# Wv's load and the clearing of z's buffer, moved in the start of a four-layer kernel

## The chip, the core and the metric

The kernel runs on one core of a Trainium2 chip. Five engines work side by side, each with its own queue: PE (TensorE) multiplies matrices, DVE (VectorE), ACT (ScalarE) and POOL (GpSimd) work on elements, and SP (SyncE) issues the transfers, which 16 DMA engines carry out. Engines wait for each other by counters (semaphores). The metric is the time of one execution on the device in microseconds; lower is better.

## The reference

Two kinds of layer, a linear attention (A) and an MLP (B), are run as A, B, A, B on 2048 tokens of 576 features, with the same weights in both turns. Weights and inputs are bf16.

```python
def _A_ref(x, wqkv, wo):              # S = 2048, D = 576, H = 32 heads of 18
    qkv = (x @ wqkv).reshape(B, S, 3, H, Dh).transpose(2, 0, 3, 1, 4)
    q, k, v = qkv[0], qkv[1], qkv[2]
    phi = lambda t: jnp.where(t > 0, t + 1, jnp.exp(t)) + 1e-6
    pq, pk = phi(q), phi(k)
    kv = jnp.einsum("bhsd,bhse->bhde", pk, v)
    z = jnp.einsum("bhsd->bhd", pk)
    num = jnp.einsum("bhqd,bhde->bhqe", pq, kv)
    den = jnp.einsum("bhqd,bhd->bhq", pq, z)[..., None] + 1e-6
    return (num / den).transpose(0, 2, 1, 3).reshape(B, S, D) @ wo

def _B_ref(x, w1, b1, w2, b2):        # F = 4608
    y = _layernorm(x, axis=-1)
    h = _gelu(jnp.einsum("bsd,df->bsf", y, w1) + b1)
    return jnp.einsum("bsf,fd->bsd", h, w2) + b2

x = A_x
x = x + _A_ref(_layernorm(x, axis=-1), A_wqkv, A_wo)
x = x + _B_ref(_layernorm(x, axis=-1), B_w1, B_b1, B_w2, B_b2)
x = x + _A_ref(_layernorm(x, axis=-1), A_wqkv, A_wo)
x = x + _B_ref(_layernorm(x, axis=-1), B_w1, B_b1, B_w2, B_b2)
```

## The kernel before

**Tiling.** Tokens go in 16 tiles of 128 (t = 0 to 15), and in four chunks of 512 for the queries. Features are cut into five pieces of up to 128 (index k). The normalised, transposed tokens stand in `yT`.

**The weights of a layer A** stand in one buffer, `wqkv_sb`, 128 partitions by 5 pieces k by 1736 columns. In each piece columns 0 to 583 hold Wq, 584 to 1159 Wk (`KO` = 584) and 1160 to 1735 Wv (`VO` = 1160). Wq is laid out in four groups of 128 columns, 126 of weights and two more, and a last group of 72 columns. The two more columns of each group are copies of the last eight of those 72: `fill_groups` (L239 to L246) makes them with two copies on POOL at L242, one over pieces 0 to 3 and 128 partitions, one over piece 4 and 64 partitions. The first product with Wq (`q_proj`, PE L708) reads such a group.

**The beginning of the first layer** is written out by hand. SP's queue: token tiles 0 to 2 (L214), Wk in two halves (L223, L225), tiles 3 and 4, Wq in five pieces (L234) and two for the last columns (L236, L238), tiles 5 to 15, and then Wv in three transfers (L223, L225 and L261: the lower half of piece 4 is loaded a second time into the upper 64 partitions). Behind these come pieces of w1 (L285), which alternate with transposes of tiles 8 to 15 by the DMA (L547). Every DMA counts on one of eight counters in turn, and waits until the DMA eight places before it, which used the same counter, has landed.

Tiles 0 to 3 are normalised on DVE, tiles 4 to 15 on POOL (L481 a power, L489, L495, in layer A one tile after the other). PE computes the keys of a tile (`k_half`, L740), ACT and DVE make pk of them (L608, L610), and PE sums, over a tile's tokens, x times pk (`rows_by_keys`, L786). Such a sum for a tile reads one more column of `pk` that POOL sets to 1 (L746). Between the tiles lie the products with Wq (`q_proj`, L708), whose results ACT and DVE turn into pq (L630, L634, L640, L642).

The hand-written order around the change is: keys of tiles 0 and 1, the sums of tile 0, keys of tile 2, `fill_groups()`, the sums of tiles 1 and 2, keys of tile 3, the first `q_proj`, the transposition of tile 4 (L558), the second `q_proj`, the sums of tile 3, and then a loop over tiles 4 to 15. Besides these orders, waits come from what the instructions read and write: an instruction that touches a region of a buffer waits for the earlier ones of the program that touch an overlapping region. The region of the first copy of L242 reaches from piece 0 to piece 3, so that columns of Wk and Wv lie inside it.

**z's buffer.** z, the sum of pk over all tokens, is collected in `zk`, which is the first of three ring buffers, `y_ring[0]`. The ring serves the first tiles' exponentials too. In `rows_by_keys` POOL clears half of `zk` at the last tile (L802, 128 by 288), and ACT writes one row into it behind that. The scheduler places this clearing on POOL's queue where its buffer is free: behind L746's columns of tiles 1 and 2 and ahead of L242.

The rest of layer A (sums for the second half of the keys, denominators, the product with Wo at L1105) and the layers B (L1220, L1216, L1284) follow in PE's order.

Of the kernel before, what the change touches and what calls it, by code (L numbers as in the profile page):

```python
# [14 lines left out]
S, D, F, H, DH = 2048, 576, 4608, 32, 18  # L15
P = 128
# [11 lines left out]
KO, VO = QW, QW + D  # L28
# [12 lines left out]
def build(tc, A_x, A_wqkv, A_wo, B_w1, B_b1, B_w2, B_b2, out, dbg=None, n_layers=4):  # L41
    nc = tc.nc
    dbg = dbg or {}
    with ExitStack() as ctx:
# [102 lines left out]
        wqkv_sb = const.tile([P, KD, QW + 2 * D], BF16, name="wqkv_sb")  # L147
# [36 lines left out]
        def chained(inst):  # L184
            if chain["last"] is not None:
                tc.add_manual_dep(inst.ins, chain["last"], NOSYNC, reason="start-up DMA issue order")
            chain["last"] = inst.ins.name
            return inst
# [30 lines left out]
        def load_wqkv(part, half=None):  # L219
            cols = slice(part * D, (part + 1) * D) if half is None else \  # L220
                slice(part * D + half * HALF, part * D + (half + 1) * HALF)
            home = slice(cols.start + QW - D, cols.stop + QW - D)
            chained(nc.sync.dma_start(out=wqkv_sb[:, 0:4, home],  # L223
                                      in_=A_wqkv[0:4 * P, cols].rearrange("(k p) n -> p k n", p=P)))
            chained(nc.sync.dma_start(out=wqkv_sb[0:64, 4, home], in_=A_wqkv[4 * P:D, cols]))  # L225
# [30 lines left out]
        load_wq()  # L256
        for t in range(5, NT):
            load_x0(t)
        load_wqkv(2)

        chained(nc.sync.dma_start(out=wqkv_sb[64:P, 4, VO:VO + D], in_=A_wqkv[4 * P:D, 2 * D:3 * D]))  # L261
        nc.vector.memset(y_ring[NY - 1][:, 0:P], 0.0)
        warm_ps = ps_h.tile([P, 512], F32, name="warm_ps", tag="h")

# [54 lines left out]
        pool_last = dict(norm=None)  # L319
# [374 lines left out]
        def layer_A(li, next_kind, pre_a1=None):  # L694
# [39 lines left out]
            zk = y_ring[0][:, 0:D]  # L734
# [38 lines left out]
            def rows_by_keys(t, half, chunks=(4, 0, 1, 2, 3), done=True):  # L773

                if t == 0 and 0 in chunks:
                    self_k["acc"] = [ps_acc.tile([P, 2, 512], F32, name="k2_ps", tag=tag) for tag in ("accA", "accB")]
                if t == 0 and 4 in chunks:
                    self_k["tail"] = ps_h.tile([P, 512], F32, name="k2_tail", tag="h")
                summed = li == 0 and half == 0
                n = HALF + summed  # L780
                pk = self_k["pk"][(0, t)][:, 0:n] if summed else \
                    self_k["pk"][(half, t // 2)][:, (t % 2) * HALF:(t % 2 + 1) * HALF]
                for k in chunks:
                    dst = self_k["tail"][0:65, 0:n] if k == 4 else self_k["acc"][k // 2][:, k % 2, 0:n]
                    lhsT = row_of[t][:, 4 * P:D + 1] if k == 4 else row_of[t][:, k * P:(k + 1) * P]
                    pe(nc.tensor.matmul(dst, lhsT=lhsT, rhs=pk, start=(t == 0), stop=(t == NT - 1)))  # L786
                cols = slice(half * HALF, (half + 1) * HALF)
                if summed and t == NT - 1:
                    for i in range(2):
                        nc.vector.tensor_scalar(out=key_eps[:, 2 * i:2 * i + 2].unsqueeze(2),  # L790
                                                in0=self_k["acc"][i][:, :, HALF:HALF + 1], scalar1=1e-6, scalar2=None,
                                                op0=ALU.mult)
                    for rows_, col in ((slice(0, 64), 4), (slice(64, 65), 5)):
                        nc.vector.tensor_scalar(out=key_eps[rows_, col:col + 1], in0=self_k["tail"][rows_, HALF:HALF + 1],
                                                scalar1=1e-6, scalar2=None, op0=ALU.mult)
                if done and t == NT - 1:
                    for i, engine in enumerate((nc.scalar, nc.vector)):
                        for j in range(2):
                            plus_eps(engine, k2[2 * i + j][:, cols], self_k["acc"][i][:, j, 0:HALF],
                                     key_eps[:, 2 * i + j:2 * i + j + 1])  # L800
                if 4 in chunks and t == NT - 1:
                    nc.gpsimd.memset(zk[:, cols], 0.0)  # L802
                    plus_eps(nc.scalar, k2[4][0:64, cols], self_k["tail"][0:64, 0:HALF], key_eps[0:64, 4:5])
                    plus_eps(nc.scalar, zk[64:65, cols], self_k["tail"][64:65, 0:HALF], key_eps[64:65, 5:6])
                if not done:
                    return
                if summed:
                    del self_k["pk"][(0, t)]
                elif t % 2:
                    del self_k["pk"][(half, t // 2)]  # L810
                if half:
                    del row_of[t]
                    if li == 0 and t == NT - 1:
                        x0_tiles.clear()
# [162 lines left out]
            if li == 0:  # L977
                def keys(t):
                    k_half(t, 0)
                    k_half(t, 1)  # L980


                def feed_and_tick(t, n):
                    feed0(t, after=dve_last["phi"] if t > 5 else None)
                    for _ in range(n):
                        lnp.tick()

                k_half(0, 0)
                lnp.tick()
                phi = k_half(0, 1, defer=True)  # L990
                k_half(1, 0)
                feed_and_tick(3, 2)
                k_half(1, 1)
                phi()
                rows_by_keys(0, 0, (0, 1, 2, 3), done=False)
                keys(2)
                fill_groups()
                feed_and_tick(4, 2)
                rows_by_keys(1, 0, (0, 1, 2, 3), done=False)
                rows_by_keys(2, 0, (0, 1, 2, 3), done=False)  # L1000
                k_half(3, 1)
                k_half(3, 0)
                q_proj(*q_left.pop(0))
                feed_and_tick(5, 1)
                feed_and_tick(6, 2)
                phi = q_proj(*q_left.pop(0), defer=True)
                lnp.tick(transposes=0)
                first_max = phi(after=first_ones["ca4"].ins.name, late=True)
                in_order("s0a s0b g0 s1a s1b n0 g1 s2a cd0 n1 s2b g2 u2 cd1 n2 ma00 s3a s3b g3 u3 ma10 ma01 n3 ma11 ma20 "
                         "s4a s4b g4 u4 ma21 ma31 s5a ma30 s5b g5 u5")  # L1010
                in_order("ln0 re0 ln1 re1 ca0 e00 ca1 e01 e10 ca2 e11 e20 e21 ca3 e31 e30 ca4")
                rows_by_keys(3, 0, (0, 1, 2, 3), done=False)
                for t in range(4, NT):
                    if t in (4, 5):
                        k_half(t, 0)
                        (first_max if t == 4 else largest)(dve_after=dve_last["phi"])
                        k_half(t, 1)
                        if t == 4:
                            in_order("u5 s6a s6b g6 u6 ma40 ma41")
                    else:  # L1020
                        keys(t)
                    pre_a1(t)
                    if t == 4:
                        lnp.tick(transposes=0)
                    masks(2)
                    if t > 4:
                        rows_by_keys(t - 1, 0)
                    else:
                        for one in range(4):
                            rows_by_keys(one, 0, (4,))  # L1030
                    behind_keys = act_last["turned"] if t <= XB or act_last["stats"] is None else act_last["stats"]
                    if t != 6:
                        largest = q_proj(*q_left.pop(0), defer=True)(after=behind_keys, late=t == 4)
                    lnp.tick(transposes=0)
                q_proj(*q_left.pop(0))
                rows_by_keys(NT - 1, 0)
                masks(len(mask_steps))
            else:
                for t in range(6, NT - TPC):
                    load_row(t)  # L1040
                for t in range(NT):

                    if t >= 4:
                        pre_a1(t)
                    k_half(t, 0)
                    if t >= 7:
                        pre_a1(t)
                    k_half(t, 1)
                    if t > 1:
                        q_proj(*q_left.pop(0))  # L1050
                    if t:
                        rows_by_keys(t - 1, 0)
                rows_by_keys(NT - 1, 0)
# [341 lines left out]
```

## Time and profile before

| | us |
|---|---|
| median of 3 runs | 763.77 (762.59 to 764.33) |
| profiled execution | 764.52 |
| span of its instructions | 762.8 |
| PE busy | 748.5 (98%) |
| PE's longest wait, for POOL's copy at L242 | 7.7 |
| ACT, DVE, POOL busy | 315.0, 261.1, 119.3 |
| DMA, share of 16 engines | 35% |

The span runs from the first to the last instruction of the core. PE's clock can be granted in part; the profile gives it as a share of full speed, 0.993 in the mean here. A timeline's row gives the start, the time, the engine, the line, the operation and, in brackets, how long the engine sat idle before it and what ended that. A row of the chain of waits gives start, time and instruction; the chain is followed back from the last instruction of the span. In a row of windows stand the stretch, its length, the busy time of PE, PE's weight loads, DVE, ACT and POOL with the number of instructions, the granted clock, the DMA's busy share and the GB/s that it moved.

### The profile page before, as it was taken

What the parts mean: (1) busy time and instruction counts of PE and PEld (TensorE: products, weight loads), DVE (VectorE), ACT (ScalarE), POOL (GpSimd) and SP (SyncE); (2) the same over time, 40 slices, a digit from 0 to 9 for tenths busy, and PEclk for the clock granted to TensorE, in tenths of its full rate; (3) what the DMA queues carried; (4) which work ended last, traced back from release to release, by engine and by line L of the source; (5) the groups of instructions that cost most, each with busy time, mean ns of one, the idle gap of its engine ahead of it and who ended that gap; (6) DMA issues with size and microseconds to landing.
All of it is one profiled execution on the core that took longest, in us unless ns stands there. A gap on an engine that the chain in (4) does not pass through costs nothing.

```text
span 762.8 us, 15695 instructions
## 1 busy us (share of the span) xinstructions
PE 748.5 (98%) x6536; PEld 475.8 (62%) x6536; DVE 261.1 (34%) x645; ACT 315.0 (41%) x703; POOL 119.3 (16%) x231
## 2 busy tenths in 40 slices
PE   6899999999999999999999999999999999999998
PEld 4566664675477447745776667447745764674476
DVE  6465764045213603300357667600240032000000
ACT  3566747403620570065037766570064036205600
POOL 2670323012100301110100004200020011001000
PEclk9799999999999999999999999999999999999999
DMA  8299496315502631230413047530241033011000
GB/s 217 80 242 227 154 274 221 83 47 158 142 19 65 183 83 40 94 87 1 141 40 86 33 126 262 205 83 16 65 107 36 16 125 82 9 32 56 2 9 24
DMA packets 88546, 75.73 MB, mean 99 GB/s; under 512 B 45002, under 2 KB 73114, under 8 KB 88474
## 3 DMA queue, kind: packets, MB, share of 16 engines
q1 hardware_dynamic: 88474, 74.72, 34.6%
q8 instruction: 51, 0.84, 0.5%
q14 instruction: 21, 0.17, 0.1%
HBM read 48.10 MB, written 24.77 MB: 96 GB/s over the span
## 4 chain that ended last, share of the span: by engine, by line
PE 93%; SPq 1%; ACT 1%; DMA 1%; DVE 1%; POOL 1%; issue 1%; POOLq 0%; ACTq 0%; DVEq 0%
PE m_ps L1284 36%; PE h_ps L1220 20%; PE hp_ps L1220 16%; PE wo_ps L1105 5%; PE q_ps L708 4%; PE k_ps L740 4%; PE k_ps L786 3%; PE m_half L1284 1%; SPq L214 1%; DMA w_sb<-in_B_w_dram 1%; PE q_ps L713 1%; DMA wqkv_sb<-in_A_wqkv_dram 1%; ACT turned L966 1%; PE k_tail L786 0%; PE rden_ps L962 0%
## 5 line engine op out<-in xcount | busy, mean ns | idle before, releaser
L1284 PE MATMUL m_ps<-w_sb,hT 128*128 128x288 bf16 x2232 | 274.8, 286 | 0.0
L1284 PEld LDWEIGHTS <-hT 128*128 128x128 bf16 x2304 | 224.3, 98 | 60.4 <-issue 3.4
L1220 PEld LDWEIGHTS <-w_sb 64*128 64x128 bf16 x2304 | 124.4, 94 | 136.7 <-issue 1.9
L1220 PE MATMUL hp_ps<-yT,w_sb 64*128 64x512 bf16 x1152 | 178.0, 376 | 0.0
L1220 PE MATMUL h_ps<-yT,w_sb 64*128 64x512 bf16 x1152 | 148.0, 376 | 0.0
L1225 ACT COPY relay_sb<-relay_sb 128x1 f32<-128x1 f32 x144 | 28.6, 199 | 260.7 <-PE h_ps L1220 218.7
L1216 ACT ACTIVATE hT<-h_ps,b1T 128x512 bf16<-128x512 f32 x144 | 91.2, 684 | 44.7 <-PE h_ps L1220 44.7
L481 POOL TENSOR_TENSOR ln_rstd<-ln_u,neg_half 128x1 f32<-128x1 f32 x62 | 34.9, 563 | 371.6 <-DVE ln_u L463 215.7
L1216 ACT ACTIVATE hT<-hp_ps,b1T 128x512 bf16<-128x512 f32 x144 | 91.2, 693 | 0.0
L684 DVE TENSOR_TENSOR xbf<-m_ps,xo 128x576 bf16<-128x576 f32 x15 | 11.4, 758 | 212.0 <-PE m_ps L1284 212.0
L684 DVE TENSOR_TENSOR xo<-m_ps,xo 128x576 f32<-128x576 f32 x16 | 12.1, 758 | 167.5 <-PE m_ps L1284 167.5
L667 POOL TENSOR_TENSOR xo<-xo,b_bc 128x576 f32<-128x576 f32 x32 | 41.0, 1284 | 105.8 <-DMA xo<-x_d 92.3
L1220 PE MATMUL h_ps<-yT,w_tail 64*128 64x512 bf16 x144 | 54.1, 376 | 0.0
L1220 PE MATMUL hp_ps<-yT,w_tail 64*128 64x512 bf16 x144 | 54.1, 376 | 0.0
L708 PE MATMUL q_ps<-yT,wqkv_sb 128*128 128x512 bf16 x160 | 41.8, 395 | 7.7 <-POOL wqkv_sb L242 7.7
L740 PE MATMUL k_ps<-wqkv_sb,yT 128*128 128x288 bf16 x320 | 44.6, 286 | 0.2 <-ACT yT L564 0.2
L1105 PE MATMUL wo_ps<-kvwo,pq 128*128 128x288 bf16 x320 | 42.3, 286 | 0.2 <-DVE xn L684 0.2
L740 PEld LDWEIGHTS <-yT 128*128 128x128 bf16 x320 | 30.9, 98 | 11.4 <-issue 0.6
L1220 PEld LDWEIGHTS <-w_tail 64*128 64x128 bf16 x288 | 27.1, 94 | 17.1
L630 ACT ACTIVATE phi_e<-q_ps 128x512 bf16<-128x512 f32 (+1 forms) x38 | 21.6, 575 | 35.4 <-PE q_ps L708 32.4
L1105 PEld LDWEIGHTS <-pq 128*128 128x128 bf16 x320 | 30.6, 98 | 8.6 <-issue 0.4
L344 DVE STREAM_TRANSPOSE turned<-y_ring 128x576 bf16<-128x576 bf16 x40 | 30.4, 767 | 0.4
(161 smaller groups left out, 546.6 us busy)
## 6 DMA issues: line engine op xcount, KB each, us to landing
xo<-x_d SPq DMA_DIRECT2D x48, 288.0 KB
x_d<-xo SPq DMA_DIRECT2D x32, 288.0 KB
xl<-x_d SPq DMA_DIRECT2D x24, 288.0 KB
y_d<-turned SPq DMA_DIRECT2D x40, 144.0 KB
w_sb<-in_B_w_dram SPq DMA_DIRECT2D x6, 864.0 KB
yT<-y_d SPq DMA_DIRECT2D x10, 512.0 KB
w_sb<-in_B_w_dram SPq DMA_DIRECT2D x9, 512.0 KB
x_d<-xn SPq DMA_DIRECT2D x16, 288.0 KB
```

The costliest lines, as they stand in the source:

```text
L344: turn = nc.vector.transpose(out=turned[:, :, j, :], in_=y[:, 0:D])
L481: power = nc.gpsimd.tensor_tensor(out=rstd[:], in0=it["u"][:], in1=neg_half[:], op=ALU.pow)
L667: nc.gpsimd.tensor_tensor(out=xo[:], in0=xo[:], in1=b2_bc[:], op=ALU.add)
L684: total = nc.vector.tensor_tensor(out=xn[:, cols].rearrange("p (h n) -> p h n", h=2), in0=halves, in1=xo[:, cols].rearrange("p (h n) -> p ...
L708: pe(nc.tensor.matmul(qp[:], lhsT=wqkv_sb[:, k, g * P:(g + 1) * P], rhs=yT[:, k, c * CA:(c + 1) * CA], start=(k == 0), stop=(k == KD - 1)))
L740: pe(nc.tensor.matmul(kp[:, 0:HALF], lhsT=yT[:, k, t * P:(t + 1) * P], rhs=wqkv_sb[:, k, KO + half * HALF: KO + (half + 1) * HALF], start= ...
L786: pe(nc.tensor.matmul(dst, lhsT=lhsT, rhs=pk, start=(t == 0), stop=(t == NT - 1)))
L1105: pe(nc.tensor.matmul(wp[:, half, 0:HALF], lhsT=features, rhs=kvwo[slot][:, half * HALF:(half + 1) * HALF], start=(g == WO_ORDER[0]), stop ...
L1216: act_last["gelu"] = nc.scalar.activation(out=to, in_=ps, func=ACT.Gelu_apprx_tanh, bias=b1T[:, f:f + 1], scale=1.0).ins.name
L1220: mm = pe(nc.tensor.matmul(dst[n], lhsT=wt, rhs=mv, start=(seen[n] == 0), stop=(seen[n] == 8)))
L1225: relay = nc.scalar.copy(out=relay_sb[:, 1:2], in_=relay_sb[:, 0:1])
L1284: pe(nc.tensor.matmul(acc[half][:, 0:cols.stop - cols.start], lhsT=hT[f][:, j * P:(j + 1) * P], rhs=w2_sb[:, f, cols], start=(f == 0), sto ...
```

## The change

Two edits. The three transfers of Wv are issued by the same queue at the same place among the transfers, but stand in the program behind `fill_groups()`, so that what they must wait for, and what must wait for them, is worked out from there. And the clearing of `zk` in the first layer gets an order: behind the last tile that POOL has normalised at that point of the program.

```diff
         for t in range(5, NT):
             load_x0(t)
-        load_wqkv(2)
-
-        chained(nc.sync.dma_start(out=wqkv_sb[64:P, 4, VO:VO + D], in_=A_wqkv[4 * P:D, 2 * D:3 * D]))
+
+        def load_wv():
+            load_wqkv(2)
+            chained(nc.sync.dma_start(out=wqkv_sb[64:P, 4, VO:VO + D], in_=A_wqkv[4 * P:D, 2 * D:3 * D]))
+
...
                 if 4 in chunks and t == NT - 1:
-                    nc.gpsimd.memset(zk[:, cols], 0.0)
+                    cleared = nc.gpsimd.memset(zk[:, cols], 0.0)
+                    if li == 0:
+                        tc.add_manual_dep(cleared.ins, pool_last["norm"], NOSYNC, reason="tiles go on first")
                     plus_eps(nc.scalar, k2[4][0:64, cols], self_k["tail"][0:64, 0:HALF], key_eps[0:64, 4:5])
...
                 keys(2)
                 fill_groups()
+                load_wv()
                 feed_and_tick(4, 2)
```

`chained` keeps the order of the transfers on SP. `load_wqkv(2)` issues two of the three transfers, for pieces 0 to 3 and for piece 4.

In the two programs' instruction lists PE, DVE and ACT have the same instructions in the same order, and so has SP; on SP the first transfer of Wv now waits for POOL as well. On POOL three things stand elsewhere: the clearing of `zk` comes behind the last mask (L113) instead of ahead of L242, and one filling of an x buffer with ones (L277) and the two L746 columns of tiles 1 and 2, which stood ahead of L242, stand behind it.

## The prediction

> **What bounds the kernel now.** The page first: PE is busy for 98% of the span, so only an idle PE, or a slow one, can give time back. The slices show both at the beginning.
>
> ```profile
> PE 748.5 (98%) x6536; PEld 475.8 (62%) x6536; DVE 261.1 (34%) x645; ACT 315.0 (41%) x703; POOL 119.3 (16%) x231
> PEclk9799999999999999999999999999999999999999
> ```
>
> The granted clock falls below full only in the second slice of 19 us. Next PE's timeline over the first 28 us, where the bracket names the wait, and POOL's over the same stretch:
>
> ```profile
> 11.98 1.15 PE L786 MATMUL k_ps<-pk,x 128*128 128x289 bf16 x8
> 12.97 1.39 PE L740 MATMUL k_ps<-wqkv_sb,yT 128*128 128x288 bf16 x10
> 22.08 2.31 PE L708 MATMUL q_ps<-yT,wqkv_sb 128*128 128x512 bf16 x5 [7.73 <-POOL wqkv_sb L242]
> ```
>
> ```profile
> 10.84 0.14 POOL L746 MEMSET pk<- 128x1 bf16 x2
> 14.74 0.34 POOL L802 MEMSET y_ring<- 128x288 bf16 x1 [3.76 <-DMA x<-in_A_x_dram]
> 21.81 0.33 POOL L242 COPY wqkv_sb<-wqkv_sb 128x32 bf16<-128x32 bf16 x2 [6.73 <-DMA w_sb<-in_B_w_dram]
> 22.11 0.54 POOL L481 TENSOR_TENSOR ln_rstd<-ln_u,neg_half 128x1 f32<-128x1 f32 x1
> ```
>
> PE stands still from 14.36 (12.97 + 1.39) to 22.08, for a copy of 0.33 us that POOL begins at 21.81. POOL is free from 15.08 and waits 6.73 us for a DMA. The row names a w1 transfer, which the copy does not touch; the name is that of the latest issue on a shared counter. Of what the copy does touch or enclose, Wv is the last. Then the windows, for the clock and the bytes:
>
> ```profile
> 16.50:17.00 0.50, 0.00 (x0) 0.00 (x0) 0.00 (x0) 0.00 (x0) 0.00 (x0) 1.00 1.07 316
> 17.00:17.50 0.50, 0.00 (x0) 0.00 (x0) 0.00 (x0) 0.00 (x0) 0.00 (x0) 0.56 0.85 277
> 26.50:27.00 0.50, 0.50 (x3) 0.22 (x2) 0.38 (x2) 0.00 (x0) 0.00 (x0) 0.50 0.00 0
> 27.00:27.50 0.50, 0.50 (x5) 0.30 (x4) 0.00 (x0) 0.40 (x1) 0.00 (x0) 0.70 0.00 0
> ```
>
> The clock halves at about 17.05, 2.7 us after PE's last matmul, and is whole again at about 27.3, 5.2 us after PE resumes. Last the chain of waits, which shows what SP waits for and what PE's slow stretch leads to:
>
> ```profile
> 3.29 4.52 DMA wqkv_sb<-in_A_wqkv_dram
> ...
> 7.83 0.82 SPq L234
> ...
> 13.38 0.43 SPq L214
> ...
> 22.08 2.31 PE q_ps L708 x5
> 24.40 0.53 PE tp L558 x5
> 24.93 2.13 PE q_ps L708 x5
> 27.07 0.67 PE k_ps L786 x4
> 27.74 0.63 PE k_ps L740 x5
> 28.36 0.02 issue
> 28.39 0.42 ACT phi_e L608
> ```
>
> Behind 28.39 the chain goes by DVE's pk and statistics and POOL's tiles to a matmul at 38.79, and stays on PE afterwards.
>
> **The change, part by part.** *When the copy can go.* In the changed program Wv's first transfer waits for POOL's copy, so the copy can't wait for Wv; it needs Wq alone. When is Wq there? From below, by bytes: token tiles 0 to 2, Wk, tiles 3 and 4 and Wq are 432 + 648 + 288 + 648 = 2016 KB by the sizes of the issues, 2064 in thousands of bytes. Windows of 2 us from 0 on moved 10, 223, 213, 275 and 239 GB/s, 1920 thousand bytes by 10.0, and 138 GB/s in the next: 2064 at 11.0. From above, by SP: a transfer waits for the one eight places ahead of it. The chain shows such a wait biting, the fifth L234 held until 7.81 for the half of Wk issued at 3.29. The eighth transfer behind the last of Wq is tile 12 at 13.38, and SP issued the eleven tiles 0.47 to 0.64 us apart without a wait: Wq had landed by 13.38. The trace's counter updates put Wq's last two landings at 11.87 and 12.10. Some updates are missing from it, so I take 12.1 as the value and 11.0 and 13.4 as ends. The second copy then ends at about 12.4, against 22.14: 9.7 us earlier.
>
> *What the copy now stands in front of.* On POOL the copies pass three small memsets, one of x (0.20) and two of pk (0.14 together); PE's sums at 11.98 read pk of tile 1. Before it was set at 10.84. Now it is set behind the copy: 12.40, x at 12.35 to 12.55, pk's first at about 12.6, PE on at 12.7, a new wait of 0.7 us. Queued behind it on PE are 8 + 10 matmuls, started 11.98 to 14.20, 2.2 us. The first product with Wq then starts at 12.7 + 2.2 = 14.9 instead of 22.08: **7.2 us**. The ends: 14.2 without any wait (7.9), 16.2 with Wq at 13.4 (5.9).
>
> *The clock.* Without the long wait PE stays at full clock. From 22.08 to the keys' end at 28.36 took 6.28. Full-speed rows of the same work: two products of five at 1.08 (the chain at 39.57), a transposition 0.28 (11.70 to 11.98), four sums 0.49 (38.92 to 39.41), five keys 0.61: 3.54, so 2.74 less. But the step after is ACT's, which first has to pass two exponents, two identity passes and the copy of tile 4; its starts lie 0.5, 0.5, 0.6 us apart at any clock, and the keys' exponent comes 3.8 us after the first product, against 6.31: **2.5 us**. Ends 2.2 (ACT a little later still) and 2.74.
>
> [...]
>
> *What follows the shift.* POOL's tile 4 is ready at 15.3 (DVE's statistics at 13.35, then 0.55 + 0.27 + 0.82 and gaps), PE asks at 16.0; tile 5, with statistics 0.7 later than the 16.2 of now, is ready at 18.9, PE asks at 19.1: hidden, narrowly. A late tile 5 would cost the difference. From 28.39 on every step hangs on the one before, so all of it moves, with its waits of 0.17 and 0.88 at 36.5 and 38.8. I leave both in; the second's loss would be 0.9 more.
>
> *SP.* Three Wv transfers are issued at 15.28, 15.75 and 16.31. Their new wait is for a copy that ends at 12.4: nothing, covered by 2.9 us. Were the copy later than 15.28, all behind it on SP (w1, the transposes of tiles 8 to 15) would wait with it. Wv itself is first read at 73.6. The transposes come 9.7 us earlier, the first at 26.0 instead of 35.7, and the DMA is done with the first transfers at 24 to 25. The gap narrows from 11 us to 1. After it w1, w2 and Wo keep their distances to PE, since the transposes pace them.
>
> *Clearing `zk`.* 0.34 us on POOL, now behind L113, which ends at 55.6. POOL has only L746's columns behind it there, which PE reads 4 us later, and is idle from 56 on; ACT's write comes at about 66. Nothing; left at its old place it would have held the copy until 15.08, some 2.7 us.
>
> *The sum.* 7.2 + 2.5 = 9.7 us off. The profiled 764.52 (span 762.8, 1.7 around it) becomes 754.8. It lies 0.75 above the median of the runs, 763.77, so against that I forecast **754.1 us**.
>
> **The rivals.** *Wq's landing or the new wait is worse.* With the copy at 13.4, the product starts at 16.2: 5.9 + 2.5 = 8.4, 755.4. For it: Wq's last columns are rows of 144 bytes, and the DMA moved only 133 to 142 GB/s from 10 to 12. Against: the landings at 11.87 and 12.10.
>
> *The new pause cools the clock.* Then the 2.5 us come back, 756.6. Against it: PE's pause of 0.88 before 38.79 leaves the clock at 1.00, and the long one held full clock for 2.7 us.
>
> *The shift is spent on the DMA.* If the transposes of tiles 8 on meet the tail of w1, keys wait. The bound is the missing gap, some 1 us, plus a transpose that is 1 us slower: 756. Against it: 4.8 us lie between the issue at 35.73 and the keys of tile 8 at 40.49.
>
> *Slower: what the copy waits for is not Wv.* If Wq's own last piece, or its counter, landed at 21.8, the copy stays, and the memsets it now stands in front of hold PE from 11.98 to 22.4. The 2.2 us of sums and keys come after the pause, and its clock is half for 5.2 us, worth 2.6 of the 2.2 + 3.54 = 5.76 us of work up to the keys; the rest takes 3.16. The keys end at 22.4 + 5.2 + 3.16 = 30.8 against 28.36: 2.4 slower, 766.2. It decides from a copy at 21.81 - 2.4 = 19.4 on. Against it: SP's issue at 13.38, and the bytes, which end Wv at about 20.1 and Wq at 11.0.
>
> *Nothing happens,* because another wait, say of the first product for its bank, ends at the same time: 763.8. Against: all five pieces of weight, yT of tiles 0 to 3 (ACT's last copy at 12.90) and the bank (tile 2's keys, read by 13.7) are there before 14.9.
>
> **How the numbers follow.** Forecast 0.72; later Wq 0.11; cooled clock 0.04; DMA 0.06; slower 0.04; nothing 0.03. The range: 7.9 + 2.74 + 0.9 = 11.5 off gives 752.3; the high end, 757.0, takes in the rivals on the faster side. Something under one in ten lies outside by these cases, and the runs of now scatter by 1.7. What can be told from no change is 0.2%, 1.5 us: faster 0.93, same 0.03, slower 0.04.
>
> **What would show it.** POOL's L242 at about 12 and its wait put down to Wq; a wait of PE before L786 of about 0.7, ended by POOL's L746; L708 at 14.9 with 1.1 us for five; no window of PE's below full clock after the first microseconds; keys of tile 4 done at 18.7. From 40 us on every row 9.7 us earlier, the first transpose on SP at 26. A wait before L740 for `yT` from tile 8 on would speak for the DMA, one before L558 for a late tile 5; L242 still past 19 would make the forecast wrong.

## The result and the profile after

The changed kernel's median is 754.26 us (753.59 to 754.7, 4 runs), that of the kernel before, with one more run than shown above, 764.05 us (762.59 to 764.5). The ratio of the two is 0.9874, with a 95% interval of 0.9857 to 0.9892: 9.6 us less, between 8.2 and 10.9. The profiled execution took 753.59 us with a span of 751.8. In the changed program the lines from 262 on are numbered two higher than in the kernel before, those from 803 on four and those past 1000 five higher: L740 is L742, L708 L710, L786 L788, L746 L748, L802 L804, L547 L549.

The page of the changed kernel, busy times and the granted clock:

```profile
PE 745.4 (99%) x6536; PEld 474.7 (63%) x6536; DVE 260.6 (35%) x645; ACT 314.1 (42%) x703; POOL 119.1 (16%) x231
PEclk9999999999999999999999999999999999999999
```

The 7 in the clock's second slice is gone. PE was busy 3.1 us less with the same 6536 matmuls, and the span is 11.0 shorter: the two ways in which time came back, speed and idle time. PE's timeline of the changed kernel:

```profile
11.56 1.41 PE L788 MATMUL k_ps<-pk,x 128*128 128x289 bf16 x8
12.81 1.39 PE L742 MATMUL k_ps<-wqkv_sb,yT 128*128 128x288 bf16 x10
14.04 1.24 PE L710 MATMUL q_ps<-yT,wqkv_sb 128*128 128x512 bf16 x5
...
15.39 1.24 PE L710 MATMUL q_ps<-yT,wqkv_sb 128*128 128x512 bf16 x5
...
26.00 1.40 PE L742 MATMUL k_ps<-wqkv_sb,yT 128*128 128x288 bf16 x10 [0.17 <-ACT yT L566]
28.33 0.28 PE L788 MATMUL k_tail<-pk,x 128*65 128x289 bf16 x1 [0.93 <-POOL pk L748]
```

The wait of 7.73 ahead of the first product is gone; that product starts at 14.04 instead of 22.08 and takes 1.24 instead of 2.31. The row at 28.33 is the matmul that stood at 38.79 in PE's timeline of the kernel before, still with its wait for POOL:

```profile
38.79 0.28 PE L786 MATMUL k_tail<-pk,x 128*65 128x289 bf16 x1 [0.88 <-POOL pk L746]
```

POOL's timeline of the changed kernel:

```profile
3.88 0.14 POOL L748 MEMSET pk<- 128x1 bf16 x2
...
11.76 0.33 POOL L242 COPY wqkv_sb<-wqkv_sb 128x32 bf16<-128x32 bf16 x2 [1.18 <-DMA wqkv_sb<-in_A_wqkv_dram]
12.03 0.20 POOL L279 MEMSET x<- 128x128 bf16 x1
12.18 0.13 POOL L748 MEMSET pk<- 128x1 bf16 x2
...
14.04 0.82 POOL L497 TENSOR_SCALAR x<-x,ln_rstd,ln_nmr 128x576 bf16<-128x576 bf16 x1
...
44.88 0.34 POOL L804 MEMSET y_ring<- 128x288 bf16 x1
```

The copy is 10.05 us earlier, and the bracket names a transfer into `wqkv_sb`. The two memsets that it now stands in front of follow at once, and the clearing of `zk` (last row) is 30 us later than it was. The row at 3.88 corrects what was said above of the columns of ones: two of them were set long before, those of tiles 0 and 1, and the two that now stand behind the copy are those of tiles 2 and 3. The chain of waits over the same stretch shows what sets the start of the first product now:

```profile
8.40 3.20 DMA wqkv_sb<-in_A_wqkv_dram
...
11.76 0.33 POOL wqkv_sb L242 x2
12.09 0.14 POOL x L279
12.23 0.08 POOL pk L748 x2
...
12.32 0.65 PE k_ps L788 x4
12.98 1.23 PE k_ps L742 x10
14.20 1.09 PE q_ps L710 x5
```

The transfer of Wq that the copy waits for lands at 11.60, the copy and the memsets pass, and the last four of PE's eight sums, those of tile 2, start at 12.32 behind the column that POOL has just set. No bracket in PE's timeline shows this wait, since it lies inside the group of eight: that group took 1.41 us, against 1.15 before, so 0.26 us.

Where the 10.9 us of this pair of profiles came back: up to the first product 22.08 - 14.04 = 8.04; from there to the matmul behind POOL's wait 16.71 us before (22.08 to 38.79) and 14.29 now (14.04 to 28.33), so 2.42 more; up to the first product of layer B 0.42 more (108.36 to 97.48 is 10.88), 0.24 of it a wait of L1105 for `xn` that is gone. After that the two run side by side.

### The profile page after: what moved, and what is told of

Its sections match the earlier page's. It is cut to its first block, busy times and chain, and to the rows that moved or that the text cites. A ratio compares the mean times of both kernels' runs of the same rounds, so it can differ in the third digit from the quotient of the medians.

```text
span 751.8 us, 15695 instructions
## 1 busy us (share of the span) xinstructions
PE 745.4 (99%) x6536; PEld 474.7 (63%) x6536; DVE 260.6 (35%) x645; ACT 314.1 (42%) x703; POOL 119.1 (16%) x231
## 4 chain that ended last, share of the span: by engine, by line
PE 94%; ACT 1%; DVE 1%; SPq 1%; POOL 1%; issue 1%; DMA 0%; POOLq 0%; ACTq 0%; DVEq 0%
PE m_ps L1289 36%; PE h_ps L1225 21%; PE hp_ps L1225 17%; PE wo_ps L1110 5%; PE k_ps L742 4%; PE q_ps L710 4%; PE k_ps L788 4%; PE m_half L1289 1%; PE q_ps L715 1%; ACT turned L970 1%; PE k_tail L788 0%; DMA wqkv_sb<-in_A_wqkv_dram 0%; PE rden_ps L966 0%; PE den_ps L922 0%; SPq L234 0%
## 5 line engine op out<-in xcount | busy, mean ns | idle before, releaser
L742 PE MATMUL k_ps<-wqkv_sb,yT 128*128 128x288 bf16 x320 | 44.5, 286 | 0.2 <-ACT yT L566 0.2
L710 PE MATMUL q_ps<-yT,wqkv_sb 128*128 128x512 bf16 x160 | 39.6, 379 | 0.0
L742 PEld LDWEIGHTS <-yT 128*128 128x128 bf16 x320 | 30.7, 98 | 11.3 <-ACT yT L566 0.7
```

What stands on the lines that cost most here:

```text
L710: pe(nc.tensor.matmul(qp[:], lhsT=wqkv_sb[:, k, g * P:(g + 1) * P], rhs=yT[:, k, c * CA:(c + 1) * CA], start=(k == 0), stop=(k == KD - 1)))
L742: pe(nc.tensor.matmul(kp[:, 0:HALF], lhsT=yT[:, k, t * P:(t + 1) * P], rhs=wqkv_sb[:, k, KO + half * HALF: KO + (half + 1) * HALF], start= ...
```

## The experiments

All times are medians; the ratio is to the kernel before, run on the same chip beside it, with medians of 763.42 to 764.05. "Product" is the start of the first product with Wq, "sum" the start of the matmul `k_tail` that waits for POOL at 38.79 in the profile of before, both from the one profiled execution of each kernel. Where the first product runs in two parts, "product" gives both.

| kernel | us | ratio (95% interval) | copy | product | sum |
|---|---|---|---|---|---|
| before | 764.05 | | 21.81 | 22.08 | 38.79 |
| changed | 754.26 | 0.9874 (0.9857 to 0.9892) | 11.76 | 14.04 | 28.33 |
| changed, run again | 753.77 | 0.9876 (0.9859 to 0.9892) | 11.73 | 14.17 | 28.46 |
| Wv's load alone | 753.93 | 0.9880 (0.9865 to 0.9895) | 11.69 | 14.15 | 28.44 |
| clearing alone | 763.65 | 1.0002 (0.9992 to 1.0011) | 21.76 | 22.03 | 37.93 |
| copy in pieces | 764.29 | 1.0009 (0.9999 to 1.0019) | 11.33, 21.11 | 14.23, 21.76 | 38.54 |
| copy and Wv in pieces | 753.88 | 0.9872 (0.9858 to 0.9887) | 11.47 | 14.10 | 28.39 |
| busy during the wait | 762.22 | 0.9985 (0.9975 to 0.9995) | 21.52 | 22.01 | 36.77 |
| Wv issued sooner | 758.29 | 0.9933 (0.9918 to 0.9947) | 16.46 | 16.73 | 32.27 |
| columns of ones first | 753.57 | 0.9871 (0.9857 to 0.9886) | 11.77 | 14.07 | 28.36 |
| and masks later | 753.69 | 0.9874 (0.9859 to 0.9889) | 11.80 | 14.02 | 27.30 |
| and fewer pieces of w1 | 753.32 | 0.9875 (0.9854 to 0.9897) | 11.69 | 13.99 | 27.27 |

### Each edit alone

Wv's load alone, the clearing of `zk` without its order:

```diff
-                    cleared = nc.gpsimd.memset(zk[:, cols], 0.0)
-                    if li == 0:
-                        tc.add_manual_dep(cleared.ins, pool_last["norm"], NOSYNC, reason="tiles go on first")
+                    nc.gpsimd.memset(zk[:, cols], 0.0)
```

> Wv's load behind the copy, the clearing of zk as before. Theory: the load alone does it; in the instruction list the clearing now falls behind tile 4's normalisation on POOL instead of ahead of the copy, so the copy still goes at about 12, the first product with Wq at about 14.1 to 14.5, and the time is within 0.5 us of the changed kernel's, about 754.3. Rival (the clearing's own move is a needed part, as the prediction's 2.7 us had it): copy at about 15.1, time 757.

POOL's timeline of this kernel:

```profile
11.69 0.33 POOL L242 COPY wqkv_sb<-wqkv_sb 128x32 bf16<-128x32 bf16 x2 [0.97 <-DMA wqkv_sb<-in_A_wqkv_dram]
...
15.16 0.34 POOL L804 MEMSET y_ring<- 128x288 bf16 x1
```

The copy goes as early as with both edits, and the time is the same. The clearing stands behind it by itself: with the copy free to go early, the scheduler queues the clearing, whose buffer is free only later, behind the copy and behind tile 4's normalisation.

The clearing alone is the kernel before with these lines of the change and without the other edit:

```diff
+                    if li == 0:
+                        tc.add_manual_dep(cleared.ins, pool_last["norm"], NOSYNC, reason="tiles go on first")
```

> The clearing of zk moved, Wv's load as before. Theory: the copy still waits for Wv's landing at 21.7, PE stands still 7.7 us, time 764.0 (ratio 0.999 to 1.001). Rival (POOL's work ahead of the copy sets its time): earlier by the clearing's 0.34 or more, up to 2.7, time 761.3 to 763.7.

It is worth nothing that these runs can tell: 763.65 us, and the interval contains 1. PE's timeline of it:

```profile
22.03 0.61 PE L708 MATMUL q_ps<-yT,wqkv_sb 128*128 128x512 bf16 x1 [8.19 <-POOL wqkv_sb L242]
...
37.93 0.28 PE L786 MATMUL k_tail<-pk,x 128*65 128x289 bf16 x1 [0.86 <-POOL pk L746]
```

The long wait stands as in the kernel before. So the whole gain is that of the load's place in the program.

### What held the copy

Wv's load stays at its old place in the program, and the copy is cut so that no single instruction's region reaches over several pieces (the clearing's order is kept):

```diff
-            for n, ks in ((P, slice(0, 4)), (64, slice(4, 5))):
+            for n, ks in [(P, slice(k, k + 1)) for k in range(4)] + [(64, slice(4, 5))]:
```

> Wv's load at its old place in the program; the copy over pieces 0 to 3 is made by four copies, each within one piece, so that none encloses columns of Wv; the clearing of zk moved as in the change. Theory (the wait was for an enclosed region, not for anything that the copy reads or writes): the copies go at about 12, time about 754.3 plus up to 0.5 for three more POOL instructions (about 0.1 to 0.2 each), ratio about 0.988. Also: SP's first Wv transfer needs no wait for POOL. Rival (Wv's place in the program matters for another reason, such as the issue of its transfers): the long wait stays, time 764.

POOL's timeline of it, and then PE's:

```profile
11.33 0.19 POOL L242 COPY wqkv_sb<-wqkv_sb 128x8 bf16<-128x8 bf16 x1 [0.48 <-DMA wqkv_sb<-in_A_wqkv_dram]
...
21.11 0.56 POOL L242 COPY wqkv_sb<-wqkv_sb 128x8 bf16<-128x8 bf16 x4 [9.38 <-DMA wqkv_sb<-in_A_wqkv_dram]
```

```profile
14.23 0.38 PE L708 MATMUL q_ps<-yT,wqkv_sb 128*128 128x512 bf16 x1
...
21.76 1.48 PE L708 MATMUL q_ps<-yT,wqkv_sb 128*128 128x512 bf16 x3 [7.16 <-POOL wqkv_sb L242]
```

The number that was expected was missed: 764.29 us, no gain. But the rows say more than a plain miss would. The copy of piece 0 went at 11.33 and PE's first matmul with it at 14.23; the other four waited until 21.11, right behind the landing of Wv at 21.06. Wv's own first transfer covers pieces 0 to 3, and its region runs from column 1160 of piece 0 to the end of piece 3. Piece 0's copy lies ahead of that region, those of pieces 1 to 3 lie inside it, and piece 4's stands behind them in POOL's queue. If that is the reason, cutting the transfer as well must free all of them:

```diff
-        load_wqkv(2)
+        for k in range(KD):
+            n = P if k < KD - 1 else 64
+            chained(nc.sync.dma_start(out=wqkv_sb[0:n, k, VO:VO + D], in_=A_wqkv[k * P:k * P + n, 2 * D:3 * D]))
```

> As the split copy, and Wv's transfer for pieces 0 to 3 is split into four, one for each piece, at its old place in the program and in SP's queue (two transfers to four and two, three more issues of 0.5 us). In the run of the split copy the copy of piece 0 went at 11.33 and those of pieces 1 to 3 at 21.11, right behind Wv's landing: a region of the transfer of Wv reaches from piece 0's columns 1160 on to piece 3's, so it still encloses the other pieces' columns of Wq. Theory (waits come from enclosed regions, on either side): with both split all copies go at about 12, the time is 753.5 to 754.8, ratio 0.987 to 0.989. Rival (Wv ahead of the copy in the program is enough for the wait): copies at 21, time 764.

POOL's timeline of the kernel with both cut:

```profile
11.47 0.69 POOL L242 COPY wqkv_sb<-wqkv_sb 128x8 bf16<-128x8 bf16 x5 [0.83 <-DMA wqkv_sb<-in_A_wqkv_dram]
```

All five copies run in one stretch at 11.47, with Wv at its old place in the program, and the time is that of the changed kernel. The wait was one for memory that only lay between, on the side of the copy and on that of the transfer.

The last test of whose landing held the copy moves the issue, not the program's order of reader and writer: in the kernel before, Wv's three transfers stand ahead of tiles 8 to 15 on SP.

```diff
-        for t in range(5, NT):
+        for t in range(5, 8):
             load_x0(t)
         load_wqkv(2)
...
+        for t in range(8, NT):
+            load_x0(t)
```

> The kernel before, with Wv's three transfers issued ahead of tiles 8 to 15 instead of behind them (1152 KB fewer ahead of it, at 280 GB/s some 4.2 us); the place of the w1 transfers is unchanged. Theory (the copy waits for Wv): copy at about 17.5, first product at about 17.8, PE's wait about 3.5 long, the clock still falls at about 17.05 and is half for about 5 us, so only the wait's part is gained: 4.2, time about 759.8 (ratio 0.9945). Rival (the copy waits for the w1 transfer that the profile names): copy at 21.8, time 764.0.

POOL's timeline of it, and then PE's:

```profile
16.46 0.33 POOL L242 COPY wqkv_sb<-wqkv_sb 128x32 bf16<-128x32 bf16 x2 [5.58 <-DMA x<-in_A_x_dram]
```

```profile
16.73 2.32 PE L709 MATMUL q_ps<-yT,wqkv_sb 128*128 128x512 bf16 x5 [2.79 <-POOL wqkv_sb L242]
...
32.27 0.28 PE L787 MATMUL k_tail<-pk,x 128*65 128x289 bf16 x1 [0.86 <-POOL pk L747]
```

The copy moved with Wv, to 16.46, although w1, which the bracket had named in the kernel before, is issued no sooner (17.69, behind the copy). Now the bracket names a tile of x. The copy reads neither: the name in a bracket for a DMA followed a shared counter here. In SP's queue of this kernel a tile of x stands eight places behind Wv's first transfer, and in that of before the first piece of w1 sixteen behind Wq's transfer of L236, each on the same one of the eight counters. The size was missed: the copy was expected at 17.5 and the time at 759.8, and the copy came 1.0 sooner and the time is 758.29. In one of the four executions, 757.04, the mean granted clock is 1.000, so there the pause hardly slowed PE, if at all; the others have 0.998.

### The clock by itself

In the kernel before, 32 products of zeros are put ahead of the first product, into the same bank, which that product then overwrites. They are work that the reference does not ask for, and keep PE busy while it waits:

```diff
                 qp = ps_h.tile([P, 512], F32, name="q_ps", tag="h")
+                for _ in range(32 if li == 0 and (g, c) == (0, 0) else 0):
+                    pe(nc.tensor.matmul(qp[:].rearrange("p (a n) -> p a n", a=4), lhsT=y_ring[NY - 1][:, 0:P],
+                                        rhs=y_ring[NY - 1][:, 0:P].unsqueeze(1).to_broadcast([P, 4, P]),
+                                        start=True, stop=True))
```

> The kernel before, with 32 matmuls of zeros into the first product's bank ahead of that product (some 0.22 us each at full clock, 6.9 together), so that PE is busy through most of its wait. Theory (two terms: the wait, and the clock behind it): the copy stays at 21.8 and the first product at 22.08, the clock stays full, the product takes 1.1 instead of 2.3, and the time falls by 2.3 to 2.7, to about 761.6 (ratio 0.9968). Rival (the half clock costs nothing because ACT, DVE or POOL set the pace behind the product): within 0.5 us of 764.0.

PE's timeline of it:

```profile
13.75 7.07 PE L707 MATMUL q_ps<-y_ring 128*128 128x512 bf16 x32
...
22.01 1.03 PE L712 MATMUL q_ps<-yT,wqkv_sb 128*128 128x512 bf16 x4 [1.19 <-DMA wqkv_sb<-in_A_wqkv_dram]
...
23.70 0.45 PE L558 MATMUL tp<-ident,x 128*128 128x128 bf16 x5 [0.66 <-POOL x L495]
...
36.77 0.28 PE L790 MATMUL k_tail<-pk,x 128*65 128x289 bf16 x1 [0.87 <-POOL pk L750]
```

PE ran at full clock (1.000 in the mean, and in every window from 14 to 30), and the kernel is 0.15% (0.05 to 0.25) faster, about 1.2 us, half of what was expected. The row at 23.70 shows one reason: the products at full speed are done before POOL has tile 4, whose normalisation stands behind the late copy, and PE waits 0.66 for it. From the product to the sum it takes 14.76 us, 0.47 more than the 14.29 of the changed kernel: so much of the clock's price can be had only with an early copy.

The rest of what is missing lies in the expected 2.4 itself, which came from one execution. The 25 executions of the kernel before that ran beside this one fall into two groups. Ten have a mean granted clock of 0.993 and take 763.67 to 764.76 us, 764.20 in the mean; fifteen have 0.996 and take 762.00 to 763.66, 762.95 in the mean. The ten of this kernel all have 1.000 and take 762.10 in the mean, 2.1 less than the first group and 0.85 less than the second. The profiles agree: the profile of before is one at 0.993, and its stretch from the product to the sum, 16.71, is 1.95 longer than here; that of the clearing alone, which has the same long wait, is one at 0.996, and its 15.90 is 1.14 longer.

### A version that beats both?

The changed kernel has two waits near the change: that for a column of ones (0.26) and that for POOL at 28.33 (0.93). First the kernel was run again as it is:

> The changed kernel unchanged, beside the next two on the same chip. Theory: ratio 0.987 to 0.988; PE's new wait before the sums of tile 2 is 0.2 to 0.4, since four sums of tile 1 lie ahead of it.

PE's timeline of this second execution:

```profile
11.96 1.15 PE L788 MATMUL k_ps<-pk,x 128*128 128x289 bf16 x8
...
14.17 1.24 PE L710 MATMUL q_ps<-yT,wqkv_sb 128*128 128x512 bf16 x5
```

The eight sums took 1.15 again, so that here the wait was nothing: PE came to them 0.40 us later and the column was there. Then the copy was ordered behind the column:

```diff
                 tc.add_manual_dep(filled.ins, first_ones["fill"].ins.name if "fill" in first_ones else pool_last["pow"], NOSYNC, reason="tiles go on first")
+                tc.add_manual_dep(filled.ins, pool_last["pk"], NOSYNC, reason="columns of ones go on first")
```

> The changed kernel with the copy ordered behind the column of ones of tile 2. Theory: the wait of about 0.3 before the sums of tile 2 is gone, the first product comes 0.2 to 0.4 earlier and the time falls by as much, about 754.0. Rival (something else holds the first product as well, Wq's last piece or the bank): no change against the changed kernel, within 0.1.

753.57 against 753.77 us: 0.2 us, which these runs don't tell apart. Next, with that order kept, POOL's masks, small operations between the tiles of the loop, start at tile 8 only:

```diff
-                    masks(2)
+                    masks(2 if t > 7 else 0)
```

> As the last one, and the masks on POOL begin at tile 8 instead of tile 4, so that four pairs of them (some 0.4 to 0.5 us a pair) leave the stretch in which PE waits 0.93 for POOL at 28.3. Theory (POOL sets the pace there): that wait falls to below 0.3 and the time by a further 0.6 to 0.9, to about 753.2 (ratio 0.9858). Rival (DVE's statistics set it, or the moved masks take it back behind tile 15): no gain over the last one.

PE's timeline of this kernel:

```profile
27.30 0.28 PE L789 MATMUL k_tail<-pk,x 128*65 128x289 bf16 x1
...
38.74 1.40 PE L743 MATMUL k_ps<-wqkv_sb,yT 128*128 128x288 bf16 x10 [0.78 <-DMA yT<-x]
...
92.51 1.39 PE L1111 MATMUL wo_ps<-kvwo,pq 128*128 128x288 bf16 x10 [0.36 <-DVE xn L687]
```

The wait of 0.93 is gone, and 0.78 of it comes back at 38.74, where the keys of tile 11 (not 12, as the next expectation has it) wait for its transposition by the DMA, and 0.36 at 92.51. The median does not move. The last step takes pieces of w1, which alternate with these transposes, out of the odd tiles:

```diff
-            for _ in range(2 if t == 4 else 0 if t == 5 else 1):
+            for _ in range(2 if t == 4 else 0 if t == 5 or t % 2 else 1):
```

> As the kernel with the copy behind the columns of ones and the masks from tile 8 on, and w1's pieces between the transposes of tiles 8 to 15 halved (every other tile; the rest follows behind tile 15). In the last run the wait of 0.93 for POOL was gone and PE lost 0.78 at tile 12's keys, for the transpose. Theory (the transposes queue behind w1's transfers): that wait is gone as well, the first product of the MLP comes at 96.8 instead of 97.6 and the time is 0.6 to 0.9 lower than the changed kernel's, ratio about 0.9865. Rival (the pieces moved behind tile 15 make Wo or the residual rows late): a new wait of PE for a DMA between 60 and 95, no gain.

PE's timeline:

```profile
74.55 0.53 PE L1111 MATMUL wo_ps<-kvwo,pq 128*128 128x288 bf16 x3 [0.98 <-POOL kvwo L877]
...
96.96 1.04 PE L1226 MATMUL h_ps<-yT,w_sb 64*128 64x512 bf16 x8
```

The wait for the DMA is gone, and one of 0.98 for POOL's `kvwo` stands at 74.55 instead. Layer B starts at 96.96, 0.45 us sooner than the 97.41 of the changed kernel in the same view, and the median, 753.32 (753.1 to 756.17), can't be told from the changed kernel's. The slowest of the four executions, 756.17, has a mean granted clock of 0.998, the others 1.000; where its clock fell no profile shows. No version here is shown to beat it.

## Why the prediction was right, step by step

*When the copy can go.* Predicted: when Wq has landed, the copy done at about 12.4. Measured: the transfer of Wq that the copy waits for at 11.60, the copy from 11.76 to 12.09. That Wv was the one waited for, and by the regions that enclose it, is shown by the two cuts and by Wv issued sooner; the rival by which the copy does not wait for Wv has fallen.

*The new wait.* It is there, but 0.26 or nothing, not 0.7. The step that failed is "PE's sums at 11.98 read pk of tile 1. Before it was set at 10.84". Tile 1's column was set at 3.88; the one behind the copy is tile 2's, which only the last four sums of the group read. By the chain it is set at 12.31, and four sums of tile 1, 0.49 us, go before. A group in a timeline has to be taken apart before a wait is put in front of it.

*The first product.* 14.04 and 14.17, against 14.9: the shift was 8.0 and 7.9, not 7.2. This is the term that was mis-sized, by 0.86 us in the first execution and 0.73 in the second. In the first PE came to the sums 0.42 sooner, at 11.56, and waited 0.44 less; in the second it came to them as predicted, at 11.96, and did not wait. Part of the 0.44 is Wq: its last two transfers landed at 11.60 and 11.80 by the trace's counter updates, against 11.87 and 12.10 in the profile of before, and the copy and the column came about 0.3 sooner with them.

*The clock.* 2.42 in the pair of profiles, 2.5 predicted. The stretch that the prediction worked out, from the first product to the exponent of tile 4's keys, took 3.82 (ACT starts that exponent at 17.86), 3.8 predicted. But the price of the slow clock is no constant. By the same distance from the product to the sum, the clearing alone, with the same long wait, took 15.90, so its cold stretch cost 1.61, and Wv issued sooner took 15.54, 1.25. The profile of before was an execution in which the cold stretch, the time of slow clock, was long: it is one of the group at 0.993, which takes 1.25 us more than the group at 0.996. That fits the two profiles' 10.9 beside the medians' 9.8. So the forecast of 9.7 is near the 9.8 partly by luck: a shift that was some 0.8 too small stood beside a clock term from a costly execution, which an average execution doesn't pay in full. That these two make up all of the difference is inferred, not shown.

How far that price varies the runs show: executions of the kernel before have a mean granted clock of 0.993 or of 0.996, and the price in three kernels' profiles was 1.25 to 2.42 us. The predicted 2.5, read from one execution at 0.993, lies just above the largest of these.

*What follows the shift.* Tile 4 was hidden narrowly: POOL had it at 14.86, PE asked at 15.12. Tile 5 caused no wait. The waits of 0.17 and 0.93 were kept, and the last three runs show what leaving them in was worth: to remove the larger one gives nothing, since another stands right behind it.

*SP and the DMA.* The first transfer of Wv, and the first transpose of SP's queue in the changed kernel:

```profile
15.06 1.29 SPq L223 DMA_DIRECT2D wqkv_sb<-in_A_wqkv_dram  x1
...
25.28 1.32 SPq L549 DMA_TRANSPOSE yT<-x  x1
```

The copy was done 3.0 us before SP came to Wv, the cover that was named. The transposes start at 25.28, 26 was predicted, and in the two half-microseconds around them the DMA had moved only 10 GB/s and nothing: the narrowed gap held. No wait of PE's matmuls at L742 names `yT` from the DMA in the changed kernel (one of a weight load does, 0.3 us); one appeared as soon as PE gained another microsecond.

*Clearing `zk`.* "Nothing" for the moved clearing is right. That at its old place it would have held the copy, for 2.7 us, is wrong: the place was taken from POOL's queue of before, but it was the scheduler's answer to a copy that had to wait anyway. With the load alone it went behind the copy.

*The rivals.* All eight executions of the changed kernel have a mean granted clock of 1.000, so the new pause did not cool it; the transposes did not meet w1; the first product did not wait for anything else. In the slower rival 2.2 + 3.54 is 5.74, not 5.76, which changes nothing.

## What to carry to other kernels

In these programs an instruction over several slices of a buffer was ordered by the region that it encloses, not by what it touches, and so was a transfer (the copies of pieces 1 to 4 at 21.11 with the copy alone cut, all five at 11.47 with both): where a small copy waits for a large load, look at what lies between the ends of both, and put the load behind its reader in the program, or cut both. PE's pause cost its length here (7.73 us of wait, and a first product 8.04 later), and in the profiles with a long one (2.79 us and more) the clock was half behind it as well; that second part varied, 1.25 to 2.42 us in three profiles, so it is taken from several profiles, or with a range. Where a wait is removed, ask which engine is a tenth of a microsecond behind: here the gain beyond the first wait went to POOL, then to the DMA, then to POOL again.

## What the runs showed of the hardware

The clock's delay was far from fixed in the four profiles with a long pause: 2.3 to 5.0 us for the fall, 2.9 to 5.8 for the return. The rows are windows of half a microsecond, with PE's last matmul of the keys before the pause ending at 14.36 (before), 13.84 (the clearing alone) and 13.94 (Wv issued sooner); first the clearing alone, then Wv issued sooner:

```profile
18.50:19.00 0.50, 0.00 (x0) 0.00 (x0) 0.00 (x0) 0.00 (x0) 0.00 (x0) 0.81 1.15 293
...
25.50:26.00 0.50, 0.50 (x3) 0.25 (x2) 0.40 (x2) 0.50 (x1) 0.23 (x2) 0.87 0.00 0
```

```profile
16.00:16.50 0.50, 0.00 (x0) 0.00 (x0) 0.00 (x0) 0.00 (x0) 0.04 (x1) 0.71 0.99 288
...
19.50:20.00 0.50, 0.50 (x4) 0.19 (x3) 0.28 (x1) 0.50 (x2) 0.39 (x2) 0.88 0.96 284
```

A clock of 0.81 over a window that starts full and ends half means a fall at 0.62 of it, at 18.81; by the same working the others are 16.21 for the fall and 25.6 and 19.6 for the return, and every window between a fall and its return has 0.50. So the clock fell 2.7, 5.0 and 2.3 us after the last matmul, and came back 5.2, 3.6 and 2.9 us after the first one behind the pause. In the copy in pieces the same working gives 2.7 for the fall and 5.8 for the return. A pause of 2.79 us, as the profile has it, was enough for the fall in three of four executions (0.998 in the mean, the fourth 1.000), while the changed kernel's 0.93 was not in any of eight (1.000).

SP's issue of Wv's first transfer took 1.29 us in the changed kernel, and 0.43 in the kernel before. The trace of the changed kernel has a 16 KB packet of the instruction queue from 14.94 on, 1.04 us long; that of the kernel before has none until 23.19, where SP issues nothing. Here the long issue, from 15.06 to 16.35, falls together with the packet. In the second execution of the changed kernel the long issue is that of Wv's third transfer (1.69 against 0.59), and in Wv issued sooner w1's two issues take 1.91 against 1.14. Whether a packet is the cause was not tried. In the changed kernel it cost nothing: the first piece of w1 started 0.65 us later, and PE did not wait for it.
